# Contracting the last pair of row blocks in two halves, scale before shift, with one no-op matmul fewer ahead of the first keys

## The chip, the cores and the metric

One core of a Trainium2 chip. The metric is the device time of one execution in microseconds. The kernel runs in about 838 us, nearly all of it back-to-back matmuls.

## The reference

An adaLN-conditioned block: linear attention, then a SwiGLU MLP, for 2048 rows of 1024. Only the conditioning and the first layernorm matter here:

```python
mod = (_silu(c) @ w_mod).reshape(c.shape[0], 6, 1, -1)
sa, ca, ga, sb, cb, gb = ...                      # six rows of 1024
h = _layernorm(x, axis=-1) * (1 + ca) + sa        # scale 1+ca, shift sa
x = x + ga * _A_ref(h, A_wqkv, A_wo)              # linear attention: kv = einsum(pk, v), ...
h = _layernorm(x, axis=-1) * (1 + cb) + sb
x = x + gb * _B_ref(h, B_w_gate, B_w_up, B_w_down)
```

The first key matmul cannot start before scale and shift are known, that is before 2 x 1024 columns of `w_mod` are loaded and contracted with silu(c).

## The kernel before

The head loads `w_mod` in pairs of row blocks (`wma[k]`, q = 1 is scale, q = 0 is shift, scale issued first), contracts each pair as it lands, in four 32-partition strips, and fills PE's spare time with no-op matmuls (`keep_warm`), meant to keep its clock up:

```python
def mod_rows_a(k):
    for j in range(k * MP, (k + 1) * MP):
        rows = wma[k][:, j % MP, :, :].rearrange("p q (i r) -> p i q r", r=P)
        for g in range(4):
            mm(mod_ps[32 * g:32 * g + 32, 0:A * 64], lhsT=sc32[:, j, :], rhs=rows[:, :, :, 32 * g:32 * g + 32],
               start=False, stop=(j == DC - 1))
# ... in the head:
    for g in range(4):
        mm(mod_ps[32 * g:32 * g + 32, 0:A * 64], lhsT=ident[:, 0:32], rhs=base_t[:, 0:A * 64], start=True, stop=False)
    nc.scalar.activation(out=scT[:], in_=mod_ps[:, A * 64:A * 64 + DC], func=ACT.Silu)
    # ... keep_warm(spare, 6); mod_rows_a(0)
    pe_transpose_tile(hT, xns[0], 0)
    keep_warm(spare, 3)
    mod_rows_a(1)
    pe_transpose_tile(hT, xns[1], 1)
    keep_warm(spare, 2)
    pe_transpose_tile(hT, xns[2], 2)
    mod_rows_a(2)
    keep_warm(spare, 5)
    mod_rows_a(3)
    keep_warm(spare, 4)
    mod_turn(0, 1)                                # DVE: turn the first block of columns
    modulate(hT, 0, ca0T, sa0T, 0, P)             # DVE: hT * scale + shift
    # ...
    k_mms(0, gs, accs, 0, 5)                      # the first keys
```

## Time and profile before

| | before |
|---|---|
| median of 6 timed runs | 837.81 us (837.55 to 838.0) |
| profile | 1249.2 us at clock 0.655 |
| profile at full clock, taken later (first experiment) | 836.2 us at clock 1.000 |

A profile's span runs from the first to the last instruction and is some 1.9 us shorter than the same execution's time. In a timeline a row is start, duration, engine, line, operation, output <- inputs, shape, count, and in brackets the idle time before it and what ended it. "issue" in brackets means that the engine waited for nothing that the profile shows.

### The profile page before, as it was taken

The numbers are of one execution on the slowest core, as the hardware profiler recorded it, in microseconds if no ns is written. First come the engines' busy times: TensorE is split into PE (matmuls) and PEld (weight loads), VectorE is DVE, ScalarE is ACT, GpSimd is POOL, SyncE is SP. The second block draws the span as 40 slices with busy tenths as digits, with TensorE's granted clock in tenths as the row PEclk, the third lists the DMA queues.
The fourth block names the chain that finished last, engine by engine and source line by source line (L and its number), as shares of the span: only waits on it lengthen the run. The fifth ranks groups of instructions, "written<-read, shape, count | busy, mean of one in ns | idle before, by whom it ended". The sixth has DMA issues, their size and how long they took to land.

```text
span 1249.2 us, 11163 instructions
## 1 busy us (share of the span) xinstructions
PE 1232.9 (99%) x4560; PEld 468.0 (37%) x4641; DVE 309.5 (25%) x598; ACT 169.3 (14%) x253; POOL 60.8 (5%) x167
## 2 busy tenths in 40 slices
PE   9999999999999999999999999999999999999998
PEld 3333333333433333333333333333333333333333
DVE  4443531564221222311111232111112221111111
ACT  2423322322011101001111000011100001111000
POOL 1101200110300001000000000000000000000000
PEclk7666666666666666666666666666666666666666
DMA  9444520139452414253140231623204218300011
GB/s 344 120 152 135 148 65 1 36 108 307 111 149 87 167 47 160 64 165 105 34 140 30 72 122 58 218 69 98 71 1 143 76 49 271 124 11 1 13 38 34
DMA packets 126756, 129.33 MB, mean 104 GB/s; under 512 B 34033, under 2 KB 108273, under 8 KB 126193
## 3 DMA queue, kind: packets, MB, share of 16 engines
q1 hardware_dynamic: 122368, 114.97, 29.3%
q0 software_dynamic: 4048, 13.25, 3.4%
q8 instruction: 36, 0.59, 0.2%
q10 hardware_dynamic: 288, 0.40, 0.1%
q14 instruction: 16, 0.12, 0.0%
HBM read 108.53 MB, written 12.72 MB: 97 GB/s over the span
## 4 chain that ended last, share of the span: by engine, by line
PE 99%; issue 1%; DVE 0%
PE acc L98 90%; PE a_ps L98 7%; PE modr L98 0%; PE kvp L98 0%; PE mod_ps L98 0%; PE tp L101 0%; PE den L98 0%; PE wf L98 0%; DVE e L638 0%; DVE ob L641 0%; DVE sel L429 0%; DVE neg_half L172 0%
## 5 line engine op out<-in xcount | busy, mean ns | idle before, releaser
L98 PE MATMUL acc<-h2T,wgu 128*128 128x512 bf16 x1756 | 580.8, 513 | 5.0 <-issue 1.6
L98 PEld LDWEIGHTS <-wgu 128*128 128x128 bf16 x1792 | 217.1, 121 | 367.4 <-issue 367.1
L98 PE MATMUL acc<-wd,gu 128*128 128x512 bf16 (+2 forms) x908 | 293.5, 503 | 2.4 <-issue 1.0
L617 DVE TENSOR_TENSOR gu<-acc,e 128x512 bf16<-128x512 f32 x112 | 77.5, 692 | 497.9 <-PE acc L98 475.4
L98 PEld LDWEIGHTS <-gu 128*128 128x128 bf16 x924 | 111.0, 121 | 182.1 <-issue 178.6
L616 ACT ACTIVATE e<-acc 128x512 f32<-128x512 f32 x112 | 66.9, 597 | 607.0 <-PE acc L98 588.5
L98 PEld LDWEIGHTS <-hT 128*128 128x128 bf16 x512 | 61.6, 121 | 102.9 <-issue 100.6
L98 PE MATMUL a_ps<-wo,pq 128*128 128x512 bf16 x250 | 85.1, 512 | 0.6
L98 PE MATMUL acc<-wk,hT 128*128 128x512 bf16 x248 | 83.7, 513 | 1.3 <-issue 0.8
L98 PE MATMUL acc<-hT,wq 128*128 128x512 bf16 x247 | 83.0, 512 | 1.6 <-issue 1.4
L98 PE MATMUL acc<-wv,hT 128*128 128x512 bf16 x251 | 83.5, 513 | 0.8 <-issue 0.4
L638 DVE TENSOR_TENSOR e<-acc,gb_bc 128x512 f32<-128x512 f32 (+2 forms) x33 | 22.3, 676 | 232.8 <-PE acc L98 219.7
L288 ACT ACTIVATE eb<-acc 128x512 bf16<-128x512 f32 x64 | 38.0, 597 | 131.8 <-PE acc L98 131.0
L289 DVE TENSOR_SCALAR eb<-eb 128x512 bf16<-128x512 bf16 x64 | 18.8, 293 | 134.0 <-ACT eb L288 133.9
L98 PEld LDWEIGHTS <-pq 128*128 128x128 bf16 x256 | 30.8, 120 | 52.6 <-issue 52.6
L98 PEld LDWEIGHTS <-wq 128*128 128x128 bf16 x256 | 29.9, 119 | 51.5 <-issue 51.2
L227 ACT ACTIVATE xn<-x,nmr,rstd 128x1024 bf16<-128x1024 f32 x16 | 19.8, 1239 | 191.9 <-POOL nmr L225 191.9
L585 POOL DMA_DIRECT2D x_scratch<-x x16 | 9.7, 608 | 657.5 <-DVE x L578 657.5
L578 DVE TENSOR_TENSOR x<-a_ps,x_sb 128x512 f32<-128x512 f32 x32 | 22.1, 692 | 35.7 <-PE a_ps L98 33.3
L326 ACT CAST v<-acc 128x512 bf16<-128x512 f32 x32 | 18.7, 584 | 57.0 <-PE acc L98 55.4
L211 POOL TENSOR_TENSOR rstd<-veps,neg_half 128x1 f32<-128x1 f32 x32 | 17.8, 555 | 103.0 <-DVE veps L209 102.9
L641 DVE TENSOR_TENSOR ob<-e,x1r 128x512 bf16<-128x512 f32 (+2 forms) x33 | 22.3, 675 | 1.0
(76 smaller groups left out, 268.4 us busy)
## 6 DMA issues: line engine op xcount, KB each, us to landing
wgu<-in_B_w_gate_dram SPq DMA_DIRECT2D x28, 1024.0 KB, 5.5
wgu<-in_B_w_up_dram SPq DMA_DIRECT2D x28, 1024.0 KB, 6.0
x_sb<-in_A_x_dram SPq DMA_DIRECT2D x32, 256.0 KB, 6.0
wml<-in_w_mod_dram SPq DMA_DIRECT2D x8, 1024.0 KB, 8.5
x_scratch<-x POOLq DMA_DIRECT2D x16, 512.0 KB, 2.9
x1r<-x_scratch SPq DMA_DIRECT2D x31, 256.0 KB, 2.8
wd<-in_B_w_down_dram SPq DMA_DIRECT2D x7, 1024.0 KB, 5.7
rbc<-rden_scratch POOLq DMA_DIRECT2D x16, 256.0 KB, 4.6
```

The costliest lines, as they stand in the source:

```text
L98: return tc.keep_in_program_order(nc.tensor.matmul(out, lhsT=lhsT, rhs=rhs, start=start, stop=stop))
L211: nc.gpsimd.tensor_tensor(out=rstd[:, 0:n], in0=veps[:, 0:n], in1=neg_half[:].to_broadcast([P, n]), op=ALU.pow)
L227: nc.scalar.activation(out=dst, in_=src, func=ACT.Identity, bias=nmr[:], scale=rstd[:, 0:1])
L288: nc.scalar.activation(out=e[:], in_=acc, func=ACT.Exp)
L289: nc.vector.tensor_scalar(out=e[:], in0=e[:], scalar1=1.0, scalar2=PHI_EPS, op0=ALU.min, op1=ALU.add)
L326: nc.scalar.copy(out=v[:, t * D + nb * NB:t * D + (nb + 1) * NB], in_=acc[:])
L578: nc.vector.tensor_tensor(out=x1[:, ns], in0=a_ps[:], in1=x_t[:, ns], op=ALU.add)
L585: nc.gpsimd.dma_start(out=x1_dram[st * P:(st + 1) * P, :], in_=x1[:])
L616: nc.scalar.activation(out=sg[:], in_=ps[0][:], func=ACT.Silu)
L617: gm = nc.vector.tensor_tensor(out=guT[sc][f // GPT][:, f % GPT, :], in0=ps[1][:], in1=sg[:], op=ALU.mult)
L638: nc.vector.tensor_tensor(out=yt, in0=y_ps, in1=gb_bc[:, ns], op=ALU.mult)
L641: nc.vector.tensor_tensor(out=ob, in0=yt, in1=x1r, op=ALU.add)
```

## The change

Intent: the scale half of the last pair lands first, so contract it while the shift half is still on its way; less PE work then remains after the landing, and one no-op fewer fits ahead of the keys.

```diff
-    def mod_rows_a(k):
+    def mod_rows_a(k, qs=slice(0, 2), last=True):
...
+            acc = mod_ps[:, 0:A * 64].rearrange("p (i q r) -> p i q r", q=2, r=32)
             for g in range(4):
-                mm(mod_ps[32 * g:32 * g + 32, 0:A * 64], lhsT=sc32[:, j, :], rhs=rows[:, :, :, 32 * g:32 * g + 32],
-                   start=False, stop=(j == DC - 1))
+                gr = slice(32 * g, 32 * g + 32)
+                mm(acc[gr, :, qs, :], lhsT=sc32[:, j, :], rhs=rows[:, :, qs, gr], start=False, stop=last and j == DC - 1)
...
-        mod_rows_a(3)
-        keep_warm(spare, 4)
+        mod_rows_a(3, slice(1, 2), False)
+        mod_rows_a(3, slice(0, 1))
+        keep_warm(spare, 3)
```

On PE that is eight matmuls more with their weight loads, and one no-op less with its own: 16 - 2 = 14 instructions more.

## The prediction

> **What bounds the kernel now.** I read the span and clock first, then the chain of waits, then the first 40 us in order of time on PE, DVE and SP, because the change touches only the first 17 us.

> ```profile
> core 0: 1249.2 us, clock 0.655
> ...
> PE 99%; issue 1%; DVE 0%
> ...
> L98 PE MATMUL acc<-h2T,wgu 128*128 128x512 bf16 x1756 | 580.8, 513 | 5.0 <-issue 1.6
> ```

> The profiled execution is not a timed one: it took 1249.2 us at a granted clock of 0.655, the timed ones 837.64 to 837.9 us. The third line gives the rate in the profile: 580.8/1756 = 331 ns from one 512-column matmul to the next. If only the clock differs, the timed runs pay 331 x 0.655 = 217 ns. Check: there are about 3700 such matmuls (1792 gate/up, some 900 down, 4 x 256 for K, V, Q and the output projection), and 3700 x 0.217 = 803 us of 837.7, so the timed runs were at full clock. I therefore use the profile for dependencies and for durations of DVE, ACT and DMA as they stand, and scale PE durations by 0.655 once PE is warm. The chain says that PE, end to end, sets the time; whatever moves the first key matmul moves the end, unless PE waits for something absolute later.

> The head of the kernel, PE in order of time (start, duration, ...):

> ```profile
> 11.91 0.86 PE L101 MATMUL tp<-ident,xn 128*128 128x128 bf16 x8
> 12.70 0.58 PE L98 MATMUL mod_ps<-wme,sc 128*32 128x384 bf16 x8
> 13.21 1.74 PE L98 MATMUL acc<-sel 128*128 128x512 bf16 x5
> 14.88 0.65 PE L98 MATMUL mod_ps<-wme,sc 128*32 128x384 bf16 x8
> 15.47 1.40 PE L98 MATMUL acc<-sel 128*128 128x512 bf16 x4
> 16.70 5.05 PE L98 MATMUL acc<-wk,hT 128*128 128x512 bf16 x15
> ```

> The lines on `sel` are the no-op matmuls. The fourth is the last pair of row blocks, and the fifth the four no-ops of which the change drops one. No line carries an idle time in brackets: in this execution PE never waits here. Beside the last two runs DVE:

> ```profile
> 15.59 0.25 DVE L271 STREAM_TRANSPOSE e<-mod_ps 128x64 f32<-128x64 f32 x1 [2.09 <-PE mod_ps L98]
> 15.88 0.57 DVE L230 TENSOR_SCALAR hT<-hT,e 128x128 bf16<-128x128 bf16 x2
> 16.36 0.51 DVE L271 STREAM_TRANSPOSE e<-mod_ps 128x320 f32<-128x320 f32 x1
> 16.91 1.54 DVE L230 TENSOR_SCALAR hT<-hT,e 128x384 bf16<-128x384 bf16 x5
> ```

> DVE waits for the last modulation matmul, turns the first block, then modulates the first keys' operand. In the instructions behind the second line the first of the two runs 15.876 to 16.190. The keys' first matmul starts at 16.70, a full 0.5 us later: at this clock the no-ops, not DVE, hold it back.

> The loads of the last pair, scale then shift (issue, kind, KB, us from issue to landing; two answers for two stretches of time):

> ```profile
> wme<-in_w_mod_dram SPq DMA_DIRECT2D x1, 384.0 KB, 7.2
> ...
> wme<-in_w_mod_dram SPq DMA_DIRECT2D x1, 384.0 KB, 7.8
> ```

> They are issued at 5.34 and 5.75, so scale lands at 12.54 and shift at 13.58. Splitting the contraction can only pay if PE gets to it between these two times.

> [...] in the trace the four of a set start 2 to 3 ns apart (12.704, 12.707, 12.710, 12.714). [...]

> **The change part by part, at full clock.**

> 1. When PE gets to the last pair. The transposes of the third tile wait for ACT's normalisation, which ends at 11.86 (10.62 + 1.24); what feeds it (DMA, DVE, POOL, a PE still cold) does not depend on the granted clock, so they begin at 11.91 here too. The next matmul came 0.79 us later in the profile: about 0.53 at full clock, so 12.44. Eight of 384 columns took 0.51 us (12.704 to 13.215): 0.33, so 12.77. Five no-ops took 1.67 us (13.215 to 14.884): 1.09, so PE stands at the last pair at 13.86. The shift landed at 13.58. So before, PE does not wait, by a margin of some 0.3 us, and the split starts nothing earlier. This margin is small against a landing of 7.8 us; if in a timed run the shift is 0.5 us later, PE waits 0.2 us before the change, and after it half of the pair's 0.38 us is done in that wait.

> 2. Cost of the split. Columns are the same: two row chunks x four strips x 384, now in twice as many instructions of 192. [...] Eight more matmuls and eight more 32-column weight loads come on top. A set of weight loads takes 92 to 95 ns in the trace[...]. As an outer bound, the kernel's one-column matmuls with a weight load each go one per 25 ns: 16 x 25 = 400 ns[...].

> 3. One no-op less. From the end of the pair (T) to the first key matmul there are two paths. PE: four no-ops from 15.466 to 16.698 = 1.23 us, at full clock 0.81, starting 0.06 before T, so T + 0.75; with three, T + 0.55. DVE: T about 15.53; start at 15.59, end of the first modulation at 16.19, and some 0.05 us to PE: T + 0.71, which no PE clock shortens. So before, the start is at the later, T + 0.75; after, at T + 0.71. Of the 0.22 us that a no-op takes, 0.04 is gained; the rest becomes an idle of PE. (At the profile's clock the no-op is worth 0.33 us and the slack of 0.5 us holds all of it.)

> 4. The next keys. The third matmul needs the second modulation (16.44 in the profile, T + 0.91) at T + 0.71 + 0.43; the seventh needs the second turn and modulation (T + 1.75) at T + 0.71 + 1.30 = T + 2.01. Both hold, with 0.2 us or more, so the gain does not return as a wait here.

> Sum: 0 (start) - 0.04 (no-op)[...], with up to 0.2 us of gain where the shift lands late. I put the centre at 0.1 us of gain.

> **Rivals.** *The DMA wait is real in the timed runs.* For it: the order scale-then-shift is the order of the loads, and there would be no reason for the split otherwise; the landing and PE's arrival are 0.3 us apart in my estimate. Against it: the profile shows no wait. It gives 837.71 - 0.2 to 0.3 = about 837.45. *A later load swallows the gain.* The DMA queues run at 9 tenths or more until 36 us, and their times are absolute. But at full clock the columns of the last two blocks are needed at about 24.0 (last load lands 23.04), the sixth key chunk at 25.5 (23.68), the values' second half at about 31 (29.68): margins of 1 us or more for a shift of 0.2. It would give exactly 837.7. *The extra instructions cost their outer bound and DVE binds:*[...] *PE's idle makes the clock fall:*[...]

> **Range and chances.** All mechanisms lie between -0.3 and +0.1 us. The three timed runs before spread over 0.26 us[...]. So 837.6, with 837.1 to 838.1 as the range. Two per cent is 16.8 us, more than the whole head, so "within 2%" is nearly certain; what is left is for a timing that falls in the throttled state that the profile was in.

> **What would show it.** In the profile after, the last pair should appear as two runs of eight 128x192 matmuls with about the same total time, then three no-ops. At a clock of 0.65 the first key matmul should come 0.2 to 0.35 us earlier than 16.70, with no idle; at full clock there should be an idle of PE of some 0.2 us before it, ended by DVE's modulation, and the first key near 15.0. Step 1 is wrong if the shift run starts well after the scale run, waiting for the load; step 2 if the two runs take over 0.1 us more than one did; step 3 if the first key follows the no-ops without a gap at full clock. The prediction fails if the timed difference is over 0.4 us either way.

(Its sum came to 0: the estimate of what the split costs stood in it against the 0.04 us of the no-op. What it takes to be the same at either clock, the traces show so: the third tile's transposes began at 11.91 us at clock 0.655, and at 11.95 and 11.92 at 1.000 (first experiment, changed kernel); the shift landed at 13.58, 13.77 and 13.63; DVE's first turn took 0.25 us and its first two modulations 0.57 in all three. PE's first nine no-ops came one per 427 ns, the last at 4.59 to 4.60, in the profile at 0.655 and in that of the changed kernel; in the former the granted clock was 1.00 until 6.68 us and 0.65 from there on.)

## More of the kernel before

For each chunk of 512 rows, between the first and the second pair of key groups, `kv_phase` multiplies keys and values in 128 tiny matmuls of 64 columns; each `mm` is two PE instructions, a weight load and a matmul (the page of the first experiment has 4641 of each):

```python
for sc in range(NSC):
    if sc > 0:
        k_phase(sc, 0, 2)
        kv_phase(sc - 1)        # 128 mm of 64 columns: 256 PE instructions
        k_phase(sc, 2, 4)       # full matmuls of 512 columns again
```

## The result, and the profile after

839.85 us median of 6 (839.75 to 840.37), against 837.81 for the kernel before. The ratio is 1.0026, 95% interval 1.0013 to 1.0039. Within 2%, but 2 us slower and outside the predicted range of 837.1 to 838.1. Both profiled executions ran at full clock; first the kernel before (the first experiment's profile), then the changed one:

```profile
core 0: 836.2 us, clock 1.000
```

```profile
core 0: 837.9 us, clock 1.000
```

The profiles differ by 1.7 us. Is it in the head? The end of the head on PE, the kernel before:

```profile
12.50 0.51 PE L98 MATMUL mod_ps<-wme,sc 128*32 128x384 bf16 x8
12.94 1.25 PE L98 MATMUL acc<-sel 128*128 128x512 bf16 x5
14.12 0.51 PE L98 MATMUL mod_ps<-wme,sc 128*32 128x384 bf16 x8
14.57 1.04 PE L98 MATMUL acc<-sel 128*128 128x512 bf16 x4
15.44 6.64 PE L98 MATMUL acc<-wk,hT 128*128 128x512 bf16 x30
```

and changed:

```profile
12.47 0.51 PE L98 MATMUL mod_ps<-wme,sc 128*32 128x384 bf16 x8
12.91 1.25 PE L98 MATMUL acc<-sel 128*128 128x512 bf16 x5
14.10 0.51 PE L98 MATMUL mod_ps<-wme,sc 128*32 128x192 bf16 x16
14.54 0.82 PE L98 MATMUL acc<-sel 128*128 128x512 bf16 x3
15.32 6.65 PE L98 MATMUL acc<-wk,hT 128*128 128x512 bf16 x30
```

The head is not slower. Sixteen half-width matmuls take about the same 0.44 us (14.10 to 14.54) as eight full ones (14.12 to 14.57), and the first key matmul comes 0.12 us *earlier*. (In the profiles of all kernels but that of experiment 7 it comes at 14.77 to 15.56, so 0.12 us between two of them does not show a gain of the change.) So the loss is later. PE's own waits for "issue" ahead of accumulating matmuls (us in total, times, longest), before and changed:

```profile
PE acc L98 <- issue: 0.4, 1, 0.4
```

```profile
PE acc L98 <- issue: 2.4, 2, 2.0
```

Where they are is shown by the chain of work that ended last (start, duration, what), first the kernel before:

```profile
61.77 1.15 PE kvp L98 x128
62.92 2.48 PE acc L98 x11
65.40 0.44 issue
65.84 25.41 PE acc L98 x117
91.26 1.15 PE kvp L98 x128
92.41 3.56 PE acc L98 x16
```

and changed:

```profile
61.66 1.15 PE kvp L98 x128
62.81 0.97 PE acc L98 x4
63.78 1.98 issue
65.76 26.92 PE acc L98 x124
92.69 1.15 PE kvp L98 x128
93.84 0.97 PE acc L98 x4
94.81 0.41 issue
```

Read the counts. PE stops a fixed number of matmuls after the burst of 128 small ones: 11 before, 4 changed, seven fewer, which is the 14 instructions more that come ahead of it. The matmul at which it stops carries no semaphore to wait for. Weight loads and matmuls counted in program order, it is number 958 in both kernels. At the second stop the weight load, number 1469, is held already; one semaphore instruction of PE lies between (at 85.2 us in the changed kernel), so the two stops are 512 PE instructions apart, 2 x 256. The sum: 1.98 - 0.44 at the first stop, 0.41 at the second, less 0.12 from the head, is 1.83 us more. The kernel before also has an idle of 0.12 us at 211 us that the changed one has not, which leaves the 1.7 us of the two spans. (These idles count from the modelled end of the matmul before, 379 ns after its start, where the next one otherwise starts after 216; so each such stop costs 0.16 us more than its figure. In this sum that cancels.)

Why 256? Both pages have this line (queue, kind: packets, MB, share),

```profile
q8 instruction: 36, 0.59, 0.3%
```

```profile
q1 hardware_dynamic: 844, 0.85, 88.3%
q8 instruction: 1, 0.02, 2.3%
```

In the trace's packets it starts at 63.06 and takes 1.08 us. So the theory (A): the burst uses up 256 instructions in 1.15 us where those of 128 full matmuls take 27.7 (experiment 4), and if it ends near the end of a block, having used up nearly all of it, PE runs dry until the next block is there. The rival (B): something in the head, or loads that the head has moved, costs the 2 us.

### The profile page after: what moved, and what is told of

Read it like the earlier page. It is cut to its first block, busy times and chain, and to the rows that moved or that the text cites. A ratio compares the mean times of both kernels' runs of the same rounds, so it can differ in the third digit from the quotient of the medians.

```text
span 837.9 us, 11258 instructions
## 1 busy us (share of the span) xinstructions
PE 829.6 (99%) x4648; PEld 378.6 (45%) x4648; DVE 308.4 (37%) x598; ACT 168.8 (20%) x253; POOL 61.0 (7%) x167
## 4 chain that ended last, share of the span: by engine, by line
PE 98%; DVE 1%; issue 0%; ACT 0%; POOL 0%
PE acc L98 90%; PE a_ps L98 7%; PE kvp L98 1%; PE modr L98 0%; DVE stats L217 0%; PE mod_ps L98 0%; PE den L98 0%; ACT xn L227 0%; DVE wo L550 0%; PE tp L101 0%; PE wf L98 0%; DVE pq L292 0%; ACT eb L289 0%; POOL rstd L211 0%; DVE mv L218 0%
## 5 line engine op out<-in xcount | busy, mean ns | idle before, releaser
L98 PE MATMUL acc<-h2T,wgu 128*128 128x512 bf16 x1792 | 387.6, 379 | 0.0
L98 PEld LDWEIGHTS <-wgu 128*128 128x128 bf16 x1792 | 175.2, 98 | 211.4 <-DMA wgu<-in_B_w_up_dram 0.3
L98 PE MATMUL acc<-wd,gu 128*128 128x512 bf16 (+2 forms) x924 | 196.1, 373 | 0.0
L98 PEld LDWEIGHTS <-gu 128*128 128x128 bf16 x924 | 89.4, 98 | 104.4
L98 PEld LDWEIGHTS <-hT 128*128 128x128 bf16 x512 | 49.4, 98 | 62.7 <-issue 4.0
L98 PE MATMUL acc<-wk,hT 128*128 128x512 bf16 x256 | 57.4, 379 | 2.4 <-issue 2.4
L98 PE MATMUL a_ps<-wo,pq 128*128 128x512 bf16 x256 | 57.4, 379 | 0.0
L98 PE MATMUL acc<-hT,wq 128*128 128x512 bf16 x256 | 56.8, 379 | 0.0
L98 PE MATMUL acc<-wv,hT 128*128 128x512 bf16 x256 | 55.9, 379 | 0.0
L98 PEld LDWEIGHTS <-pq 128*128 128x128 bf16 x256 | 25.0, 98 | 30.2
L98 PEld LDWEIGHTS <-wq 128*128 128x128 bf16 x256 | 24.5, 98 | 29.9 <-issue 0.9
```

The lines of the kernel that those rows point to most:

```text
L98: return tc.keep_in_program_order(nc.tensor.matmul(out, lhsT=lhsT, rhs=rhs, start=start, stop=stop))
```

## The experiments

All kernels gave correct results. A "tick" is a no-op matmul of one column (two PE instructions, about 25 ns: the kernel's own one-column matmuls start 25 ns apart, from 23.58 us on in the changed kernel), placed where PE waits for data anyway:

```python
def tick(acc, n):
    for _ in range(n):
        mm(acc[:, 0:1], lhsT=sel[:, 0, :], rhs=sel[:, 0, 0:1], start=True, stop=True)
```

**1. The kernel before, for a profile at full clock.** No edit.

> The kernel before, unchanged, for a profile at full clock. What it is to settle: where the changed kernel's 2.0 us come from. In the changed kernel's trace PE stands still from 63.4 to 65.8 us (1.98 us) and for 0.41 us at 94.8 us, in the middle of a run of key matmuls and with no semaphore to wait for; both times just after a kv burst (256 PE instructions in 1.15 us), and both at PE instruction number 958 plus a multiple of 256. Theory A (instruction supply): PE's instructions come in blocks of 256; a burst that fills nearly a whole block uses it up before the next block is there. Before the change the burst lies 14 instructions (7 matmuls) further from the block's end, so PE has 7 x 0.216 = 1.5 us more of work there: I expect a stall of about 0.5 us at the first kv burst, none at the second, the first key matmul within 0.2 us of the changed kernel's 15.32, and 837.8 us. Theory B (the head): no-op and split cost 2 us, or shift the loads so that PE waits later: then the first key matmul comes more than 1 us earlier than 15.32, or the stall at 63 us is there with the same length in both.

837.98 us. The profile is the one shown above: first stop 0.44 us, second none, first key at 15.44. A holds. B needed a head over 1 us shorter or the same stop in both.

**2. The kernel before with the changed kernel's numbering.**

```diff
         keep_warm(spare, 2)
+        tick(spare, 7)
```

> The kernel before, without any of the change, but with seven one-column no-op matmuls (14 PE instructions) where PE waits for the third tile's normalisation anyway. This gives PE the changed kernel's numbering from there on. A: stalls as in the changed kernel, about 2.0 and 0.4 us, time 839.7 (839.3 to 840.2). B: seven small matmuls in an idle stretch cost nothing, 837.8.

839.82 us, ratio 1.003 (1.0017 to 1.0042). Stops of 2.04 and 0.81 us, each four matmuls after the burst (the second twice as long as in the changed kernel, see "Left open"). Fourteen idle instructions, with nothing of the change, reproduce its loss. Two of the five runs took 841.35 and 841.61; the profile is the latter, and its windows (stretch, length, busy time of PE, PEld, DVE, ACT, POOL, granted clock, DMA share, GB/s) say why:

```profile
63.00:66.00 3.00, 0.96 (x6) 0.33 (x4) 0.40 (x2) 0.00 (x0) 0.00 (x0) 1.00 0.36 118
66.00:69.00 3.00, 3.00 (x9) 1.08 (x8) 0.98 (x2) 0.60 (x1) 0.00 (x0) 0.50 0.03 8
```

The clock column falls to 0.50: after the stop some eight matmuls come one per 427 ns instead of 216, a further 1.7 us.

**3. The changed kernel with the numbering of the one before.**

```diff
-        for g in range(4):
-            mm(mod_ps[32 * g:32 * g + 32, 0:A * 64], lhsT=ident[:, 0:32], ...
+        mm(mod_ps[:, 0:A * 64], lhsT=ident[:], rhs=base_t[:, 0:A * 64], start=True, stop=False)
...
-        keep_warm(spare, 3)      # after the first tile's transposes
+        keep_warm(spare, 1)
...
-        keep_warm(spare, 2)
```

> The changed kernel with 14 PE instructions taken out ahead of the head's end: the four base matmuls as one of 128 columns (same values, 6 instructions), and four no-ops left out where PE then waits for data anyway (8 instructions). The PE numbering is that of the kernel before. A: the first stall falls to about 0.5 us, the second is gone, 837.8 (837.3 to 838.2). B: the head is still the changed one, 839.8 or more.

837.72 us, ratio 1.0001 (0.9988 to 1.0013). One stop of 0.43 us, eleven matmuls after the burst; none at the second. (The five runs spread from 837.17, the profiled one, to 839.02, that one at a granted clock of 0.998.) With split and dropped no-op in place, the loss is gone.

**4. The changed kernel with the burst moved well into a block.**

```diff
         keep_warm(spare, 2)
+        tick(spare, 22)
```

> The changed kernel with 22 one-column no-ops (44 PE instructions) in the same idle stretch: the kv burst now starts 36 instructions into a block, so that PE has 18 full matmuls (3.9 us) and most of the burst in it before it needs the next block, over the 4.0 us that the changed kernel's trace shows from the block's first instruction to its successor (1.15 + 0.86 + 1.98). A: no stall at either place, 837.4 (837.0 to 837.9), although the kernel has more instructions than any before. B: 839.8 to 840.4.

837.04 us (836.81 to 837.71), ratio 0.9991 (0.9979 to 1.0004). No stop:

```profile
61.68 1.15 PE kvp L98 x128
62.83 27.73 PE acc L98 x128
90.57 1.15 PE kvp L98 x128
```

The block's packet now starts at 56.31, over 5 us ahead of the burst. The kernel has 44 instructions more and is the fastest so far.

**5. The burst filling a block from end to end.**

```diff
         keep_warm(spare, 2)
+        tick(spare, 4)
```

> The changed kernel with four one-column no-ops (8 PE instructions) in the idle stretch, so that the kv burst's 256 instructions fill a block from end to end and none of the four full matmuls (0.86 us) that followed it in the block is left. A (a block is used up before its successor is there): both stalls grow by about 0.9 us, the first to 2.8, the second to 1.3, time 841.5 (841.0 to 842.2), more where the longer idle makes PE fall to half rate, as it did in the profile of e2_before_pad7 at 66 us. Rival (any shift of the changed kernel's numbering helps, or four tiny matmuls do nothing): 839.8 or less.

842.83 us (842.5 to 843.33). The stop is where and as long as expected:

```profile
61.04 1.22 PE L98 MATMUL kvp<-v,pk 128*32 128x64 bf16 x128
65.11 5.08 PE L98 MATMUL acc<-wk,hT 128*128 128x512 bf16 x15 [2.85 <-issue]
```

2.85 us at the first, 1.38 at the second. For the second the profile names a load, not "issue":

```profile
97.11 3.63 PE L98 MATMUL acc<-wk,hT 128*128 128x512 bf16 x16 [1.38 <-DMA wml<-in_w_mod_dram]
```

That load landed at 97.09, but it is not what this matmul needs: in the changed kernel the same matmul, the first after the burst, ran at 93.77, and that load landed at 95.80. The time is 1.3 us over the central expectation and outside its range; in the profile some eight matmuls at half rate follow the stop (1.7 us), which the expectation had named as a possible extra, and all five runs have a granted clock of 0.997 or 0.998.

**6. The kernel before with the numbering of experiment 4.**

```diff
         keep_warm(spare, 3)
+        tick(spare, 10)
...
         keep_warm(spare, 2)
+        tick(spare, 19)
```

> The kernel before with 29 one-column no-ops (58 PE instructions) in two idle stretches of the head, so that its PE numbering from the head's end on is that of e4_after_pad22, which had no stall. A: no stall at the kv bursts, 837.2 (836.9 to 837.6); against e4 (837.04) this leaves what the change does in the head by itself, 0.1 us by the first key matmul of the two profiles (15.44 before, 15.32 after). Rival (e4 was fast because of the change): 837.8.

837.10 us, no stop, first key at 15.41 (15.34 in experiment 4). So the gain of 4 was not the change's. With the stops out of both, before and changed stand at 837.10 and 837.04: what the change is worth by itself is 0.07 us in these two profiles, below what timing resolves.

**7. A whole block more.**

```diff
+        tick(spare, 13)     # after keep_warm(spare, 3)
...
+        tick(spare, 115)    # after keep_warm(spare, 2)
```

> The changed kernel with 128 one-column no-ops, 256 PE instructions, a whole block. They cost 128 x 25 ns = 3.2 us less some 0.8 us of idle that they fill. A, with blocks of 256: the place of the burst in its block is unchanged, so both stalls stay, at the same place behind the burst (four full matmuls after it), and the time is 842.2 (841.5 to 843). Rival (an absolute count or an absolute time matters, not the place in a block): the stalls vanish or move, 840 to 840.5.

```profile
65.57 1.22 PE L98 MATMUL kvp<-v,pk 128*32 128x64 bf16 x128
66.72 1.04 PE L98 MATMUL acc<-wk,hT 128*128 128x512 bf16 x4
69.88 0.38 PE L98 MATMUL acc<-wk,hT 128*128 128x512 bf16 x1 [2.12 <-issue]
```

Four matmuls, then 2.12 us, though the burst is 256 instructions and 4 us later; the second stop is 0.38. What counts is the place in a block of 256, as A says. The time, 844.38 us (842.96 to 846.77), missed my expectation of 842.2 (841.5 to 843): I had put the ticks at 2.4 us net, and the first key came 4.0 us later. After 115 one-column matmuls PE fell to half rate: the no-ops from 15.6 to 17.3 us are 427 ns apart.

**8. A candidate to beat both.** Experiment 3's single base matmul and 25 ticks for the numbering of experiment 4.

```diff
-        for g in range(4):
-            mm(mod_ps[32 * g:32 * g + 32, 0:A * 64], lhsT=ident[:, 0:32], ...
+        mm(mod_ps[:, 0:A * 64], lhsT=ident[:], rhs=base_t[:, 0:A * 64], start=True, stop=False)
...
+        tick(spare, 10)     # after keep_warm(spare, 3)
...
+        tick(spare, 15)     # after keep_warm(spare, 2)
```

> A candidate to beat both: the changed kernel with the four base matmuls as one of 128 columns (in e3_after_less7 the SiLU of c then came at 5.12 instead of 5.84, and the first key at 14.89 instead of 15.32) and 25 one-column no-ops for the PE numbering of e4_after_pad22. A: no stall at the kv bursts and a head 0.3 to 0.4 us shorter, 836.7 (836.3 to 837.1). Rival (the earlier SiLU in e3 was the phase of PE's warm-up, as it varied between profiles anyway): 837.0, as e4.

837.01 us (836.88 to 837.26), ratio 0.9991 (0.998 to 1.0003): the rival's number. No stop, but the first key came at 15.30, not at 14.9. The SiLU that starts the head's chain came at 5.56 here, at 5.12 in experiment 3, and at 5.21 to 5.84 in the nine profiles whose base was still four matmuls; it goes with when PE reaches full rate in an execution (in the traces' clock record at 4.04 us in experiment 3, at 4.94 here, and at 5.96 to 6.29 in the five profiles whose SiLU comes at 5.84). The shorter head of experiment 3 was mostly that. What then set the first key in both was the load of the shift half: it landed at 13.79 in experiment 3 and at 14.21 here, PE started on it 0.04 us later, and the first keys are the same 0.42 us apart.

**9. The dropped no-op alone.**

```diff
         mod_rows_a(3)
-        keep_warm(spare, 4)
+        keep_warm(spare, 3)
```

> One part of the change alone: the kernel before with three no-ops instead of four ahead of the first keys, the last pair not split. Two PE instructions fewer, so one full matmul (0.22 us) more between burst and block end. A: the first stall falls from 0.44 to about 0.2 us, none at the second; the first key comes about 0.1 us earlier after the last pair's end, as in the changed kernel; time 837.5 (837.1 to 837.9). Rival (the dropped no-op is what costs 2 us): 839.8.

837.37 us, ratio 0.9997 (0.9983 to 1.0011). One stop, 0.35 us (0.2 was expected), twelve matmuls after the burst. Here the shift half landed late, at 14.29 us (13.77 in experiment 1), and PE did wait for it:

```profile
14.34 0.51 PE L98 MATMUL mod_ps<-wme,sc 128*32 128x384 bf16 x8 [0.17 <-DMA wme<-in_w_mod_dram]
14.78 0.82 PE L98 MATMUL acc<-sel 128*128 128x512 bf16 x3
15.56 1.68 PE L98 MATMUL acc<-wk,hT 128*128 128x512 bf16 x7
```

So the wait that the split is meant for exists, in some executions. And there the split does what it is meant for: in experiments 3, 5, 8 and 10 PE came to the pair before the shift half had landed, did the scale half, and waited between the halves for 0.07 to 0.26 us more. In experiment 3 the pair therefore takes 0.71 us to the next no-op (14.11):

```profile
13.40 0.78 PE L98 MATMUL mod_ps<-wme,sc 128*32 128x192 bf16 x16
```

In these four the pair ends some 0.32 us after the landing, in experiment 9, unsplit, 0.49 after it: some 0.17 us of the head gained when the load is late. No timing here resolves that.

**10. The split alone.**

```diff
         mod_rows_a(3, slice(1, 2), False)
         mod_rows_a(3, slice(0, 1))
-        keep_warm(spare, 3)
+        keep_warm(spare, 4)
```

> The other part alone: the changed kernel with its fourth no-op put back. Sixteen PE instructions more than before. A: stalls as in the changed kernel and one matmul longer, about 2.2 and 0.6 us, and a first key 0.1 us later than there; 840.3 (839.8 to 841), more in runs that fall to half rate. Rival (split and no-op act together): 837.8.

841.92 us (840.26 to 842.66), ratio 1.0049 (1.0036 to 1.0062). Stops of 1.94 and 0.80 us, three matmuls after the burst. The first is 0.2 us shorter than expected; in the profile some eight matmuls at half rate follow it. The median is over the expected range, but four of the five runs have a granted clock of 0.998; the one at 1.000 took 840.26, as expected. (The traces of 9 and 10 lack about every 49th matmul record; the counts allow for that.) The split is what costs, by its sixteen instructions.

All together, by what PE has left in the block after the burst:

| kernel | full matmuls left | first stop | second stop | median us |
|---|---|---|---|---|
| 5 | 0 | 2.85 | 1.38 | 842.83 |
| 10 | 3 | 1.94 | 0.80 | 841.92 |
| changed | 4 | 1.98 | 0.41 | 839.85 |
| 2 | 4 | 2.04 | 0.81 | 839.82 |
| 7 (one block later) | 4 | 2.12 | 0.38 | 844.38 |
| before (1) | 11 | 0.44 | 0 | 837.98 |
| 3 | 11 | 0.43 | 0 | 837.72 |
| 9 | 12 | 0.35 | 0 | 837.37 |
| 4, 6, 8 (block ends inside the burst) | - | 0 | 0 | 837.04, 837.10, 837.01 |

The medians of 5, 7 and 10 also hold half rate. The kernel has two more such bursts, the third and the fourth; in the changed kernel the first two start at 180 modulo 256, these at 244 and 52, and in none of the profiles does PE stop behind them. From 0 to 4 matmuls the first stop falls by 0.87 us, from 4 to 11 by 1.54; at 0.216 us each these are 0.86 and 1.51. Whatever work lies between, PE goes on 3.9 to 4.3 us after the first burst's start: 65.84 - 61.70 in the kernel before, 65.76 - 61.59 changed, 65.11 - 61.04 in experiment 5, 69.88 - 65.57 in 7. No record shows PE waiting for the packet, so that link is inferred; but in all 13 stops of the table PE goes on 1.3 to 1.6 us after the end of the packet that came last.

## Why the prediction was wrong, point by point

- **What bounds the kernel: right, with one wait overlooked.** PE sets the end, and what moves the first key moves the end "unless PE waits for something absolute later". I went through the data loads for such a wait, with margins of 1 us and more, and those held. I did not think of PE's own instructions as a load.
- **Step 1, PE's arrival at the last pair: right in kind.** Predicted 13.86 with the shift landed at 13.58; in the changed kernel 14.10 and 13.63. Most of the difference is the factor 0.655 on two durations: a set of eight took 0.44 us, not 0.33, five no-ops 1.19, not 1.09. No wait in the profiles of the kernel before and the changed one; one of 0.17 us in experiment 9, and waits between the halves in experiments 3, 5, 8 and 10. The margin was rightly called small, and the gain that the prediction saw in a late landing was there. (A slip: the starts that it quotes for the four strips are 3 to 4 ns apart, not 2 to 3.)
- **Step 2, cost of the split: the step that failed.** As the prediction put it: "Eight more matmuls and eight more 32-column weight loads come on top", with 400 ns for all sixteen as an outer bound (its finer estimate is cut). Locally they made no measurable difference: the pair took 0.44 us in both profiles. What failed is that it charged the sixteen instructions only where they run. They also shift the number of everything behind them (by 14, with the dropped no-op), and that cost 1.54 + 0.41 us of PE standing still behind the two bursts. Experiments 2 (shift without change) and 3 (change without shift) settle it, 5 and 10 give the dose, 7 the period.
- **Step 3, the no-op: mechanism right, both paths some 0.1 us too short.** The two paths were put at T + 0.75 and T + 0.71. In the profile before, four no-ops fill the time from the pair's end to the first key (14.57 to 15.44, 0.87 us = 4 x 0.216); changed, it is 0.78 for three (0.65), so now DVE's path ends last, at T + 0.78 rather than 0.71, and PE loses 0.12 us there. Dropping one gains 0.09 rather than 0.04, and not by chance: the seven profiles with three no-ops all have 0.77 to 0.78 here, the four with four all 0.87 to 0.88. The rest of the 0.12 us earlier first key is a head that was 0.03 earlier already.
- **Step 4, the next keys: right.** The 30 key matmuls take 6.65 us in one run, as before (6.64).
- **Rivals.** None was the cause. "The extra instructions cost their outer bound" named the right objects and the wrong cost. "PE's idle makes the clock fall" was dismissed, for the head rightly: with an idle of 0.12 us there the granted clock of the changed kernel was 1.00 from 12 to 16 us. Later it did happen: behind stops of 2.04, 2.85 and 1.94 us in experiments 2, 5 and 10 the clock column is at 0.50 for some 3.4 us (from 66.0, 65.6 and 66.1), but behind those of 1.98 us in the changed kernel and 2.12 in experiment 7 it stays at 1.00. The length of the stop alone does not tell them apart. What does in these five profiles is where it lies: the granted clock changed only at whole multiples of 3.413 us after PE reached full rate (in the changed kernel at 6.281 and, at the end, at 839.133, 244 of them later), and between two such points the idle was 2.04, 2.85 and 1.94 us where the clock fell, at most 1.46 (changed kernel, whose stop spans the point at 64.31) and 1.80 (experiment 7) where it did not. In the head of experiment 7 it fell, at 14.94 us, behind 115 one-column matmuls and without such a stop. "The DMA wait is real" was true of five of the later profiles, but it is not what cost 2 us.
- **The range** was built from the spread of the timed runs and the terms of the sum. It left out that a step of the kernel far from the change was on an edge: the kernel before already lost 0.44 us there, in the middle of a phase that looked solid. The slow profile that I had could not show it: at clock 0.655 burst and eleven matmuls last 86.15 to about 91.1, 5 us, more than the 4 us that the block takes to come.

Left open: why the first burst's block takes 4 us and the second's 2.6 to 3.0 (95.22 - 92.62 changed, 97.08 - 94.07 in experiment 2). The traces narrow it to the start of the packet: 1.4 to 1.7 us after the first burst's start, 0.2 after the second's in the changed kernel and in experiments 5 and 7, but 0.7 in experiment 2 and 0.5 in experiment 10, whose second stops are 0.8. What delays the start stays open. Also open is why two of the changed kernel's six timed runs took 0.5 us more than the other four. That the medians differ by 2.04 us and the profiles by 1.7 comes of the executions that were profiled: 838.03 for the kernel before, 0.22 over its median and with the idle at 211 us, and 839.75 for the changed one, 0.10 under its own.

## What to carry to other kernels

Where PE issues a burst of tiny matmuls in a row, here 128 in 1.15 us, look at their place in PE's instruction stream: in this kernel that place, modulo 256, set a stop of 0 to 2.85 us behind the first burst. Edits ahead of it that change the number of PE instructions move it: without touching the burst the change lost 2 us so, and experiments 4, 6 and 8 gained 0.7. No other kernel was tried. If a small edit moves the time by more than its work, look for a PE idle without a releaser and count instructions; then shift the stream with a few cheap no-ops in an idle stretch before judging the edit; 22 to 29 of them cost nothing measurable here, 128 delayed the first key by 4.0 us. They bring either kernel to about 837.05 us, some 0.7 us better than the kernel before, and leave 0.06 us between the two; each of these ratios' intervals alone just includes 1.
